# Batch 1's query scaling on VectorE alone, masked-score products in two passes around the fence, and a first matmul pair ahead of block 0's second-half outputs

## The chip, the cores and the metric

The kernel runs on one core of one Trainium2 chip. That core has five engines with a queue of their own each: TensorE (PE, whose weight loads are listed as PEld), VectorE (DVE), ScalarE (ACT), GpSimd (POOL) and SyncE (SP, which here issues nearly all DMAs). An engine works through its instructions in program order and waits for the others by semaphores. The metric is the device time of one execution in microseconds (us), lower is better; the kernel before takes 295.61 us (median of three runs).

## The reference, cut to what matters

A retention layer without a softmax (8 batches, 8 heads, 576 positions, head size 64), whose output is fed to a two-layer network with the activation h * sigmoid(beta * h):

```
gamma = 1 - 2 ** (-5 - arange(H))
Dmat  = where(i >= j, gamma[h] ** (i - j), 0)          # i, j: positions
attn  = ((q @ k.T) / sqrt(64) * Dmat) @ v              # per batch and head
x     = attn, rows (batch, position), columns (head, 64)   # 4608 x 512
h     = x @ w_in                                       # 512 -> 2048
out   = (h / (1 + exp(-beta * h))) @ w_out             # 2048 -> 512
```

## The kernel before, in words

The decay gamma ** (i - j) is split into a factor on the query row (`gq`), a factor on the value row (`gv`, `gvh`) and a 0/1 mask. Queries multiplied by `gq` are called `qs`, values multiplied by their factor `vn`, keys cast to bf16 `kn`. The sequence of a batch is cut into chunks of 64 positions. Inside a chunk the kernel forms masked scores `R` (TensorE product in PSUM, then a VectorE multiplication by the mask, line 493) and multiplies them with `vn`. Everything before the chunk comes in through a running state of 64 x 64 per head: products of `kn` and `vn` (line 504), summed chunk by chunk on VectorE (line 512), cast to bf16 (`sbd`, `sbq`, `end`) and multiplied with the transposed queries `qT`. Both contributions are accumulated in the same PSUM banks `O`, which are then copied to `xT`, the transposed input of the network.

The work stands in nine blocks of 512 rows: one for the first 512 positions of each batch u = 0 to 7, and one (u = 8 in the attention code) for the last 64 positions of all eight batches. A block's network part is 64 `up` matmuls (lines 719 and 734, into `ph`, each group ending in an activation on ScalarE into `gT`) and 64 `down` matmuls (line 754, into `po`), all 128 x 128 by 512 columns. The attention part of a later block is threaded between the network matmuls of an earlier one.

The order is written out by hand. `merged` takes a list `fill` of steps, mostly groups of network matmuls, and streams of pairs (place in the list, step); before step n of `fill` it issues all stream steps whose place is at most n. The order of issue is the program order of every engine; nothing reorders it later. Three places matter here.

**Block 0's second half.** Block 0's own attention runs first, from line 790 on. Its output has two halves, pairs of heads 0 and 1 and pairs 2 and 3. `s_cross(c, a)` (line 418) adds the state's part of half a with two 128 x 128 by 128 matmuls, and `s_x` (line 425) copies one bank of the half to `xT`, one on ScalarE and one on VectorE. The function `rest` (line 846) issues `s_cross` for chunks 1 to 3 of half 1 (six matmuls), both copies, two casts of `w_in` and a reciprocal. It stands at place 1, after the first step of `fill`. That step, `ups(0, (0, 1), 0, ...)`, has four network matmuls which read half 0 of `xT`; the next step has four more on half 0, and the third, `ups(0, (0, 1), 1, ...)`, is the first that reads half 1.

**Batch 1's queries.** `pre_q(b, n)` (line 279) makes a quarter of `qs`. Calls n = 0 and 1 take heads 0 to 3 and n = 2 and 3 heads 4 to 7, each for two of the four position groups. For batch 1 the calls 2 and 3 consist of two instructions each, for even and odd heads, because the heads are exchanged in pairs (`turned`, line 274). All are on VectorE but the second one of n = 3, which is on GpSimd. Then `t_q(1, 0)` and `t_q(1, 1)` (line 343) transpose `qs` on TensorE, eight transposes each, and a copy (line 348) gives `qT`. GpSimd's next instructions are the casts of batch 1's first keys (`o_pre`, line 574).

**The outputs of blocks 2 to 8.** `d_out(u)` (line 519) issues 64 matmuls of 64 x 64 by 64 with `R` and `vn` (line 533), called the own products here, and then the state's part in two halves, `cross(0)` and `cross(1)` (line 546), 28 matmuls each (32 in u = 8). The four 64 x 64 tiles of TensorE work side by side. The own products and `cross(0)` write any given region of `O` from one and the same half of the array's rows, `cross(1)` from the other half. So `cross(1)` must not run into own products that are still on their way into the same region. A fence does that: a one-column VectorE memset (line 537) waits for the last own product, and the first two matmuls of `cross(1)` wait for the memset:

```
        fence = nc.vector.memset(fenced[:], 0.0)
        after(fence, last)
```

For u = 2 to 6, `outputs` (line 955) puts the 32 state matmuls of the next block (`d_st`) between `cross(0)` and `cross(1)`; it does so while the block is built, by running `d_out`, then `chain = d_st(u + 1, 0)`, and then `cross(1)`. For u = 7 and u = 8 nothing stands between them. Block 1's second half has an output function of its own, `half_out` (line 676), in which the own products already stand in two passes of 16 with the fence behind the first pass.

Of the kernel before, what the change touches and what calls it, by code (L numbers as in the profile page):

```python
# [19 lines left out]
def kernel(  # L20
# [10 lines left out]
    nc = tc.nc  # L31
# [5 lines left out]
    HP = H // 2  # L37
# [3 lines left out]
    CB = MB // P  # L41
# [28 lines left out]
    QB = 1  # L70
    HT = MB // 2
    VB = 4
    q_tiles, kv_tiles = {}, {}
# [92 lines left out]
    for x in range(2):  # L166
        t = causal_span[x * D:(x + 1) * D]
        nc.gpsimd.affine_select(out=t, in_=t, pattern=[[-1, 2], [1, CB], [CB, PC]], compare_op=ALU.is_ge,
                                fill=0.0, base=0, channel_multiplier=-2)
# [8 lines left out]
    fenced = consts.tile([P, 1], F32, name="fenced")  # L178
# [28 lines left out]
    def cast_w_in(g, kos=None, pool=()):  # L207
        t = wts[g]
        f0, fn, rows = pieces[g]
        for ko in kos or range(rows[0].start, rows[-1].stop):  # L210
            if ko % 2 == 0 or ko in pool:
                nc.gpsimd.tensor_copy(w_in_sb[:, ko, f0:f0 + fn], t[:, ko])  # L212
                continue
            nc.vector.tensor_copy(w_in_sb[:, ko, f0:f0 + fn], t[:, ko])
# [48 lines left out]
    def xt(m):  # L263
        if m not in xts:
            xts[m] = xpool.tile([P, HP, CB, P], BF16, name="xT", tag="xT" if m < B else "xTt", bufs=2 if m < B else 1)
        return xts[m]

    state_ps = {}
    batch, pair, live, vns = {}, {}, {}, {}
# [4 lines left out]
    turned = [(slice(0, HP), slice(0, HP)), (slice(HP, H, 2), slice(HP + 1, H, 2)), (slice(HP + 1, H, 2), slice(HP, H, 2))]  # L274

    def head_of(b, p, j):
        return 2 * p + (j if b is not None and b < QB or p < 2 else 1 - j)

    def pre_q(b, n):

        if n == 0:
            batch[b] = dict(qs=sb.tile([P, CB, H, D], BF16, name="qs", tag="qs", bufs=2),
                            qT=sb.tile([P, CB, HP, P], BF16, name="qT", tag="qT", bufs=2))
        if b < 2:
            hs, cs = slice(n // 2 * HP, (n // 2 + 1) * HP), slice(n % 2 * 2, n % 2 * 2 + 2)
            for e, (to, hs) in zip((nc.vector, nc.gpsimd if n == 3 else nc.vector), [(hs, hs)] if n < 2 or b < QB else turned[1:]):
                e.tensor_tensor(batch[b]["qs"][:, cs, to], q_tiles[b][:, hs, cs].rearrange("p h i d -> p i h d"),  # L287
                                        gq[:, cs, hs].unsqueeze(3).to_broadcast([P, 2, len(range(H)[hs]), D]), ALU.mult)
        else:
            if n % 2:  # L290
                return
            cs = slice(n, n + 2)
            for to, hs in turned:
                nc.gpsimd.tensor_tensor(batch[b]["qs"][:, cs, to], q_tiles[b][:, hs, cs].rearrange("p h i d -> p i h d"),  # L294
                                        gq[:, cs, hs].unsqueeze(3).to_broadcast([P, 2, len(range(H)[hs]), D]), ALU.mult)
# [54 lines left out]
    spread = [(0, 0), (1, 1), (0, 1), (1, 0)]  # L350

    def half(x):
        return slice(x * D, (x + 1) * D)
# [64 lines left out]
    def s_cross(c, a):  # L418

        for pl in range(2):  # L420
            p = 2 * a + pl
            nc.tensor.matmul(s_view(s_Os[a][c % 2][:, c // 2, pl, :]), sbds[c - 1][:, p, :], s_q(c, slice(0, P), p),
                             start=False, stop=True, skip_group_check=True)

    def s_x(a, hh, e):
        e(xt(0)[:, 2 * a:2 * a + 2].rearrange("k p i (s h w) -> k (p i) s h w", s=2, h=2)[:, :, :, hh, :],
          s_Os[a][hh].rearrange("k s p (i w) -> k (p i) s w", i=CB))
# [30 lines left out]
    def piece(u, c):  # L458

        return live[u * CB + c // 2]  # L460

    def q_of(u, c, j, p):

        if u == B:
            return piece(u, c)["qkT"][half(j), 0, p, half(c % 2)]
        w = TL // CB
        return batch[u]["qT"][half(j), :, p, c * w:(c + 1) * w]

    def columns(u, o):
        return o if u == B else o.rearrange("k (i s) -> k i s", i=CB)  # L470

    def after(later, earlier):
        tc.add_manual_dep(later.ins, earlier.ins.name, mybir.DependencyInfo(mybir.DependencyClass.Sync, mybir.DependencyReason.DATA))
# [45 lines left out]
    def d_out(u):  # L519

        shape = [P, 2, CB, TL] if u == B else [P, 2, CB, CB, TL // CB]
        O = {(hh, y): psum.tile(shape, F32, name="O", tag="sc" if y else "O", bufs=2) for y in range(2) for hh in range(2)}

        def to(c, p, x):
            o = O[c % 2, p // 2][half(x), p % 2]
            return o[:, c // 2] if u == B else o[:, :, c // 2]

        R = batch[u]["R"]
        for cc in range(CB):
            for p in range(HP):  # L530
                for hh, j in spread:
                    h = head_of(u, p, j)
                    last = nc.tensor.matmul(to(2 * cc + hh, p, h % 2), piece(u, 2 * cc)["vn"][half(hh), h, :],  # L533
                                            columns(u, R[cc // 2][half(hh), j, cc % 2, p, :]),
                                            start=cc == 0 and p % 2 == 0, stop=False, skip_group_check=True)

        fence = nc.vector.memset(fenced[:], 0.0)
        after(fence, last)

        def cross(flip):  # L540
            for n, (cc, pp, y, j) in enumerate((cc, pp, y, j) for cc in range(CB) for pp in range(2) for y in range(2) for j in range(2)):
                c, p = 2 * cc + (j ^ flip), pp + 2 * y
                if u < B and c == 0:
                    continue
                s = ends[c] if u == B else sbq[c - 1]
                m = nc.tensor.matmul(to(c, p, j ^ y), s[half(j), p, :], q_of(u, c, j, p),  # L546
                                     start=False, stop=True, skip_group_check=True)
                if flip and n < 2:
                    after(m, fence)

        cross(0)

        def evict():
            for n, ((hh, y), o) in enumerate(O.items()):
                x = xt(u)[:, 2 * y:2 * y + 2]
                if u == B:
                    x, o = x[:, :, :, half(hh)].rearrange("k p c q -> k (p c) q"), o.rearrange("k p c q -> k (p c) q")
                else:
                    x = x.rearrange("k p i (c h s) -> k (p i) c h s", c=CB, h=2)[:, :, :, hh, :]
                    o = o.rearrange("k p i c s -> k (p i) c s")  # L560
                (nc.scalar.copy if n % 2 else nc.vector.tensor_copy)(x, o)  # L561
        return lambda: cross(1), evict
# [159 lines left out]

    phs = {}

    def ups(m, fs, u, banks):

        if m not in gts:
            gts[m] = sb.tile([P, FO, CB, P], BF16, name="gT", tag="gT", bufs=2)
        if u == 0:
            for f, tag in zip(fs, banks):  # L730
                phs[f] = psum.tile([P, MB], F32, name="ph", tag=tag, bufs=dict(mm=3, O=2, sc=2, st=1)[tag])
        kos = (2 * u, 2 * u + 1)
        for ko, f in [(ko, f) for ko in kos for f in fs] if u == 0 or len(fs) == 2 else [(ko, f) for f in fs for ko in kos]:
            nc.tensor.matmul(phs[f][:], w_in_sb[:, ko, f * P:(f + 1) * P], xts[m][:, ko],  # L734
                             start=(ko == 0), stop=(ko == KO - 1))
            if ko == KO - 1:
                nc.scalar.activation(gts[m][:, f], phs[f][:], ACT.Silu, scale=beta_sb[:, f:f + 1])  # L737
# [46 lines left out]
    def F(f, *a):  # L784
        return lambda: f(*a)
# [60 lines left out]
    def rest():  # L846
        for c in range(1, CB):
            s_cross(c, 1)
        s_x(1, 0, act)
        s_x(1, 1, dve)  # L850
        cast_w_in(1, (2, 3))
        nc.vector.reciprocal(rbeta_sb[:], beta_sb[:])
# [5 lines left out]
    def last_state():  # L858
        for a in range(2):
            s_keep(a, 3, (dve, dve), 1 - a)  # L860

    fill = [F(ups, 0, (fo, fo + 1), u, tags) for u in range(2) for fo, tags in ((0, ("mm", "mm")), (2, ("O", "O")))]
    fill += [F(ups, 0, (4, 5), u, ("sc", "sc")) for u in range(2)]
    fill += [F(up, 0, fo) for fo in (6, 7)]
    for fo, tags in ((8, ("O", "O", "sc", "sc")), (12, ("mm", "mm", "mm", "st"))):
        for u in range(2):
            fill += [F(ups, 0, range(fo, fo + 4), u, tags), lambda: None]
    d0 = len(fill)
# [50 lines left out]
    def triangles():  # L919
        for t, pattern in zip(tri, ([[1, CB], [CB, TL // CB]], [[1, TL]])):  # L920
            nc.gpsimd.memset(t[:], 1.0)
            for x in range(2):
# [1 line left out]
                nc.gpsimd.affine_select(out=t[w], in_=t[w], pattern=pattern, compare_op=ALU.is_ge,  # L924
                                        fill=0.0, base=0, channel_multiplier=-1)

    streams = [[(d0 + 2, F(triangles)), (1, rest), (2.5, F(last_products)), (3.6, F(last_state))], [(0, F(load_w_out, 0)), (1.6, F(cast_w_in, 2)), (2.1, F(cast_w_in, 3)), (2.2, F(load_w_out, 1)),
                (4.1, F(cast_w_in, 4)), (6.1, F(cast_w_in, 5)), (6.2, F(load_w_out, 2)), (8.1, F(cast_w_in, 6)),
                (10.1, F(cast_w_in, 7)), (10.2, F(load_w_out, 3))],
               [(d0 - 4 + 3.3 * g, F(cast_w_out, g)) for g in range(WG)],  # L930
# [100 lines left out]
```

## Time and profile before

| | us |
|---|---|
| median of three runs | 295.61 (295.37 to 295.71) |
| the profiled execution, own time | 295.49 |
| its span on the core | 293.8 |
| TensorE matmuls busy | 284.9 (97%) |
| VectorE busy | 104.9 (36%) |
| ScalarE busy | 145.9 (50%) |
| GpSimd busy | 110.5 (38%) |

Times in the trace count from the start of the span. The profiled execution took 295.49 us, 1.7 us more than its span, and 0.12 us less than the median. A line of the timeline gives the start, the time from the first start to the last end, the engine, the source line, the operation, the tiles written and read, the shape and the number of instructions merged into it. Matmuls are pipelined, so that one lasts longer than the distance to the next; distances between starts are what counts on TensorE. The records of some matmuls are missing (55 of the 56 of line 734 are there).

### The profile page before, as it was taken

Reading aid. Unit: us, or ns where it says so; the run is one execution under the profiler, and the core shown is the slowest. Engines: PE = TensorE matmul, PEld = TensorE weight load, DVE = VectorE, ACT = ScalarE, POOL = GpSimd, SP = SyncE. Lnnn points to the kernel's source line nnn. Section 1 sums busy time; section 2 is a strip of 40 time slices with the busy share of each in tenths; the row PEclk is TensorE's granted clock in tenths of the full one; section 3 lists DMA queues with packets and bytes.
Section 4 is the critical chain, followed back from the end, with each engine's and each line's share of the span. In section 5 each row is a group of like instructions: output and inputs, shape, how many; then the busy total and the mean of one; then the engine's idle time right before and its main releaser. Section 6 shows DMA issues by size and latency. Waiting matters only on the chain.

```text
span 293.8 us, 7934 instructions
## 1 busy us (share of the span) xinstructions
PE 284.9 (97%) x3373; PEld 147.1 (50%) x3404; DVE 104.9 (36%) x222; ACT 145.9 (50%) x262; POOL 110.5 (38%) x220
## 2 busy tenths in 40 slices
PE   7899999999999999999999999999999999999995
PEld 2554456885544554455445544554554544444443
DVE  5864566606620650065104520453053500110012
ACT  5556537882387335743473348434780168007600
POOL 3956047944730924371329505773313000000000
PEclk9999999999999999999999999999999999999999
DMA  7999999999999999939999949989997110131011
GB/s 226 305 367 386 377 271 268 209 154 241 231 150 253 271 203 242 243 63 167 229 238 211 185 123 249 193 177 208 208 164 138 74 38 0 36 71 38 0 71 71
DMA packets 121986, 53.99 MB, mean 184 GB/s; under 512 B 97744, under 2 KB 114400, under 8 KB 121952
## 3 DMA queue, kind: packets, MB, share of 16 engines
q1 hardware_dynamic: 121920, 53.49, 82.6%
q8 instruction: 26, 0.43, 0.6%
q14 instruction: 8, 0.07, 0.1%
q10 hardware_dynamic: 32, 0.01, 0.0%
HBM read 36.71 MB, written 9.44 MB: 157 GB/s over the span
## 4 chain that ended last, share of the span: by engine, by line
PE 84%; DMA 10%; SPq 3%; issue 1%; DVE 1%; POOL 0%
PE po L754 39%; PE ph L719 37%; DMA qn<-in_q_dram 4%; DMA wt<-in_moe_w_out_dram 3%; DMA wt<-in_moe_w_in_dram 2%; SPq L104 2%; PE sc L486 2%; PE O L533 2%; PE st L504 1%; PE O L546 1%; DVE qs L287 1%; SPq L204 1%; PE ph L886 0%; SPq L84 0%; PE sc L609 0%
## 5 line engine op out<-in xcount | busy, mean ns | idle before, releaser
L754 PE MATMUL po<-w_out_sb,gT 128*128 128x512 bf16 (+2 forms) x573 | 125.1, 373 | 2.4 <-issue 2.1
L721 ACT ACTIVATE gT<-ph,beta_sb 128x512 bf16<-128x512 f32 (+1 forms) x144 | 91.4, 643 | 48.3 <-PE ph L719 47.9
L719 PE MATMUL ph<-xT,w_in_sb 128*128 128x512 bf16 (+1 forms) x566 | 113.1, 356 | 0.5
L754 PEld LDWEIGHTS <-gT 128*128 128x128 bf16 x593 | 56.1, 98 | 63.9
L719 PEld LDWEIGHTS <-w_in_sb 128*128 128x128 bf16 x576 | 56.0, 98 | 55.1 <-DVE first L512 0.3
L761 DVE COPY ot<-po 128x512 f32<-128x512 f32 (+2 forms) x33 | 22.2, 672 | 72.8 <-PE po L754 70.0
L493 DVE TENSOR_TENSOR R<-sc,tri 128x512 bf16<-128x512 f32 x30 | 18.7, 683 | 61.5 <-PE sc L486 61.5
L294 POOL TENSOR_TENSOR qs<-qn,gq 128x256 bf16<-128x256 f32 (+1 forms) x36 | 26.4, 763 | 36.9 <-DMA qn<-in_q_dram 36.9
L323 POOL CAST kn<-kvn 128x128 bf16<-128x128 f32 (+1 forms) x78 | 22.8, 331 | 31.4 <-DMA kvn<-in_k_dram 31.3
L301 POOL TENSOR_TENSOR vn<-kvn,gv 128x512 bf16<-128x512 f32 x26 | 27.0, 1044 | 6.3 <-DMA kvn<-in_v_dram 6.0
L561 ACT CAST xT<-O 128x512 bf16<-128x512 f32 x14 | 7.5, 589 | 31.9 <-PE O L546 31.9
L516 ACT CAST sbd<-warm 128x256 bf16<-128x256 f32 x18 | 7.3, 405 | 25.7 <-DVE warm L512 20.7
L734 PE MATMUL ph<-xT,w_in_sb 128*128 128x512 bf16 x55 | 12.9, 379 | 0.1
L512 DVE TENSOR_TENSOR warm<-st,first 128x256 f32<-128x256 f32 x20 | 8.4, 422 | 9.6 <-PE st L504 8.4
L512 DVE TENSOR_TENSOR first<-st,warm 128x256 f32<-128x256 f32 x25 | 10.6, 425 | 2.5
L561 DVE CAST xT<-O 128x512 bf16<-128x512 f32 x14 | 9.0, 686 | 4.9 <-PE O L546 4.9
L737 ACT ACTIVATE gT<-ph,beta_sb 128x512 bf16<-128x512 f32 x14 | 8.7, 687 | 4.2 <-PE ph L734 4.2
L311 POOL TENSOR_TENSOR kn<-tln,gq 128x128 bf16<-128x128 f32 (+1 forms) x12 | 5.7, 471 | 11.8 <-DMA tln<-in_q_dram 6.5
L212 POOL CAST w_in_sb<-wt 128x256 bf16<-128x256 f32 (+1 forms) x15 | 8.0, 546 | 4.9 <-DMA wt<-in_moe_w_in_dram 4.9
L516 ACT CAST sbd<-first 128x256 bf16<-128x256 f32 x18 | 7.3, 405 | 2.3 <-DVE first L512 0.3
L734 PEld LDWEIGHTS <-w_in_sb 128*128 128x128 bf16 x56 | 5.2, 98 | 6.3 <-issue 0.5
L229 DVE TENSOR_SCALAR w_out_sb<-wt,rbeta_sb 128x512 bf16<-128x512 f32 x13 | 5.9, 484 | 5.0 <-DMA wt<-in_moe_w_out_dram 5.0
(132 smaller groups left out, 166.4 us busy)
## 6 DMA issues: line engine op xcount, KB each, us to landing
qn<-in_q_dram SPq DMA_DIRECT2D x16, 512.0 KB, 6.2
kvn<-in_k_dram SPq DMA_DIRECT2D x32, 256.0 KB, 5.8
kvn<-in_v_dram SPq DMA_DIRECT2D x32, 256.0 KB, 5.3
out_dram<-ot SPq DMA_DIRECT2D x31, 256.0 KB, 3.6
wt<-in_moe_w_out_dram SPq DMA_DIRECT2D x8, 512.0 KB, 9.2
wt<-in_moe_w_in_dram SPq DMA_DIRECT2D x5, 512.0 KB, 10.2
wt<-in_moe_w_in_dram SPq DMA_DIRECT2D x6, 256.0 KB, 6.9
tln<-in_q_dram SPq DMA_DIRECT2D x8, 128.0 KB, 4.6
```

Source lines behind the costliest of these rows:

```text
L294: nc.gpsimd.tensor_tensor(batch[b]["qs"][:, cs, to], q_tiles[b][:, hs, cs].rearrange("p h i d -> p i h d"), gq[:, cs, hs].unsqueeze(3).to_ ...
L301: nc.gpsimd.tensor_tensor(live[i]["vn"], kv_tiles.pop(i)[:, 1], gains(gv, c), ALU.mult)
L323: nc.gpsimd.tensor_copy(kn[:, c % 2, to], t[:, 0, hs])
L493: nc.vector.tensor_tensor(R[x][:, j].rearrange("k c p q -> k (c p) q"), sc[x, j].rearrange("k c p q -> k (c p) q"), mask, ALU.mult)
L512: nc.vector.tensor_tensor(new[:], add, sums[(c - 1) % 2][:], ALU.add)
L516: e((sbq[c] if c < NC - 1 else ends[u])[:], new[:])
L561: (nc.scalar.copy if n % 2 else nc.vector.tensor_copy)(x, o)
L719: nc.tensor.matmul(ph, w_in_sb[:, ko, fo * P:(fo + 1) * P], xts[m][:, ko, :, w], start=(ko == 0), stop=(ko == KO - 1))
L721: nc.scalar.activation(gts[m][:, fo, :, w], ph, ACT.Silu, scale=beta_sb[:, fo:fo + 1])
L734: nc.tensor.matmul(phs[f][:], w_in_sb[:, ko, f * P:(f + 1) * P], xts[m][:, ko], start=(ko == 0), stop=(ko == KO - 1))
L754: nc.tensor.matmul(po[:, x:y], gT[:, fo, ms, :], w_out_sb[:, fo, n0 + x:n0 + y], start=(fo == 0), stop=(fo == FO - 1), skip_group_check=m < 2)
L761: (nc.scalar.copy if m == 0 else nc.vector.tensor_copy)(ot, po[:, :nn])
```

## The change

It has three parts.

1. In `pre_q`, all scaling instructions of batches 0 and 1 go to VectorE. One instruction moves: the last of batch 1, 128 x 256 elements, from GpSimd to VectorE.
2. In `d_out`, the 64 own products are issued in two passes of 32. The first pass has the products whose regions `cross(1)` will write, the second those that `cross(0)` will write. The fence stands between the passes. `cross` is unchanged.
3. The first step of `fill` is split: two of its four matmuls, then `rest`, then the other two. `ups` gets an argument `one` for that. The rest of the order stays.

```
@@ pre_q
-            for e, (to, hs) in zip((nc.vector, nc.gpsimd if n == 3 else nc.vector), [(hs, hs)] if n < 2 or b < QB else turned[1:]):
-                e.tensor_tensor(batch[b]["qs"][:, cs, to], q_tiles[b][:, hs, cs].rearrange("p h i d -> p i h d"),
+            for to, hs in ([(hs, hs)] if n < 2 or b < QB else turned[1:]):
+                nc.vector.tensor_tensor(batch[b]["qs"][:, cs, to], q_tiles[b][:, hs, cs].rearrange("p h i d -> p i h d"),
@@ d_out
-        for cc in range(CB):
-            for p in range(HP):
-                for hh, j in spread:
-                    h = head_of(u, p, j)
-                    last = nc.tensor.matmul(to(2 * cc + hh, p, h % 2), piece(u, 2 * cc)["vn"][half(hh), h, :],
-                                            columns(u, R[cc // 2][half(hh), j, cc % 2, p, :]),
-                                            start=cc == 0 and p % 2 == 0, stop=False, skip_group_check=True)
-
-        fence = nc.vector.memset(fenced[:], 0.0)
-        after(fence, last)
+        for other in range(2):
+            for n in range(32):
+                cc, pp, y, hh = n // 8, n // 4 % 2, n // 2 % 2, n % 2
+                p, j = pp + 2 * y, hh if other else 1 - hh
+                h = head_of(u, p, j)
+                last = nc.tensor.matmul(to(2 * cc + hh, p, h % 2), piece(u, 2 * cc)["vn"][half(hh), h, :],
+                                        columns(u, R[cc // 2][half(hh), j, cc % 2, p, :]),
+                                        start=cc == pp == 0, stop=False, skip_group_check=True)
+            if not other:
+                fence = nc.vector.memset(fenced[:], 0.0)
+                after(fence, last)
@@ ups
-    def ups(m, fs, u, banks):
+    def ups(m, fs, u, banks, one=None):
-        if u == 0:
+        if u == 0 and not one:
-        kos = (2 * u, 2 * u + 1)
+        kos = (2 * u, 2 * u + 1) if one is None else (2 * u + one,)
@@ fill and streams
-    fill = [F(ups, 0, (fo, fo + 1), u, tags) for u in range(2) for fo, tags in ((0, ("mm", "mm")), (2, ("O", "O")))]
+    fill = [lambda: (ups(0, (0, 1), 0, ("mm", "mm"), 0), rest(), ups(0, (0, 1), 0, None, 1))]
+    fill += [F(ups, 0, (fo, fo + 1), u, tags) for u, fo, tags in ((0, 2, ("O", "O")), (1, 0, None), (1, 2, None))]
-    streams = [[(d0 + 2, F(triangles)), (1, rest), (2.5, F(last_products)), (3.6, F(last_state))], ...
+    streams = [[(d0 + 2, F(triangles)), (2.5, F(last_products)), (3.6, F(last_state))], ...
```

More of the change, by code (lines that the diff above doesn't have):

```diff
@@ L925, in triangles @@
                                         fill=0.0, base=0, channel_multiplier=-1)
-    streams = [[(d0 + 2, F(triangles)), (1, rest), (2.5, F(last_products)), (3.6, F(last_state))], [(0, F(load_w_out, 0)), (1.6, F(cast_w_in, 2)), (2.1, F(cast_w_in, 3)), (2.2, F(load_w_out, 1)),
+    streams = [[(d0 + 2, F(triangles)), (2.5, F(last_products)), (3.6, F(last_state))], [(0, F(load_w_out, 0)), (1.6, F(cast_w_in, 2)), (2.1, F(cast_w_in, 3)), (2.2, F(load_w_out, 1)),
                 (4.1, F(cast_w_in, 4)), (6.1, F(cast_w_in, 5)), (6.2, F(load_w_out, 2)), (8.1, F(cast_w_in, 6)),
```

## The prediction, made before the changed kernel had run

> **What bounds the kernel.** I read the page's busy shares first, then the list of waits, then the timeline at the three places that the change touches.
>
> ```profile
> PE 284.9 (97%) x3373; PEld 147.1 (50%) x3404; DVE 104.9 (36%) x222; ACT 145.9 (50%) x262; POOL 110.5 (38%) x220
> ...
> PE T L347 <- DVE qs L287: 1.2, 4, 0.4
> ```
>
> TensorE is busy for 97% of the span, and its longest listed wait for another engine after the start is the 0.4 us for `qs` at the transposes of line 347. So a saving counts only where TensorE itself stops, and such stops are short. They have to be read from distances between starts, because the modelled ends hide them.
>
> Place one, block 0's second half, on TensorE:
>
> ```profile
> 15.76 1.04 PE L734 MATMUL ph<-xT,w_in_sb 128*128 128x512 bf16 x3
> 16.63 0.50 PE L422 MATMUL O<-qT,sbd 128*128 128x128 bf16 x6
> 16.97 2.06 PE L734 MATMUL ph<-xT,w_in_sb 128*128 128x512 bf16 x8
> 18.96 0.44 PE L439 MATMUL st<-vn,kn 64*64 64x64 bf16 x16
> 19.33 2.76 PE L734 MATMUL ph<-xT,w_in_sb 128*128 128x512 bf16 x12
> 21.93 0.38 PE L719 MATMUL ph<-xT,w_in_sb 128*128 128x512 bf16 x1
> ```
>
> From 19.33 to 21.93 twelve matmuls take 2.60 us, 0.217 each. From 16.97 to 18.96 eight take 1.99, where 8 x 0.217 = 1.73, plus some 0.10 for the turn to small matmuls (77.14 to 77.44 is 0.30 for one matmul and such a turn), gives 1.83: a stop of about 0.16. It lies before the third step, which needs half 1 of `xT`; VectorE's copy of that half runs from 17.17 to 17.86, when the eight are half done.
>
> Place two, batch 1's queries:
>
> ```profile
> 40.09 0.43 DVE L287 TENSOR_TENSOR qs<-qn,gq 128x256 bf16<-128x256 f32 x1 [0.25 <-DMA qn<-in_q_dram]
> 40.20 0.79 POOL L287 TENSOR_TENSOR qs<-qn,gq 128x256 bf16<-128x256 f32 x1 [11.28 <-DMA qn<-in_q_dram]
> 40.43 0.84 DVE L287 TENSOR_TENSOR qs<-qn,gq 128x256 bf16<-128x256 f32 x1
> 41.00 0.73 POOL L574 CAST kn<-kvn 128x512 bf16<-128x512 f32 x1
> 41.19 0.82 DVE L287 TENSOR_TENSOR qs<-qn,gq 128x256 bf16<-128x256 f32 x1
> ...
> 40.93 0.83 PE L347 MATMUL T<-ident,qs 128*128 128x128 bf16 x12
> 42.16 0.38 PE L347 MATMUL T<-ident,qs 128*128 128x128 bf16 x4 [0.40 <-DVE qs L287]
> ```
>
> TensorE issues twelve transposes and stops for the last four until VectorE's third instruction ends at 42.01; they begin 0.15 later, at 42.16. Four transposes take 0.22 (42.16 to 42.38), twelve 0.65, so TensorE could have gone on at about 41.59: the stop is 0.57. VectorE's start is set by the queries' landing, which also ended GpSimd's wait of 11.28.
>
> Place three, the fence, in u = 7 and u = 8:
>
> ```profile
> 218.00 0.71 PE L533 MATMUL O<-R,vn 64*64 64x64 bf16 x64
> 218.54 0.38 PE L546 MATMUL O<-qT,sbd 64*64 64x64 bf16 x23
> 218.81 0.06 DVE L537 MEMSET fenced<- 128x1 f32 x1 [2.20 <-PE O L533]
> 218.92 0.40 PE L546 MATMUL O<-qT,sbd 64*64 64x64 bf16 x24
> ...
> 231.93 0.83 PE L546 MATMUL O<-kT,end 64*64 64x64 bf16 x64
> 232.21 0.06 DVE L537 MEMSET fenced<- 128x1 f32 x1 [0.88 <-PE O L533]
> 232.92 0.59 PE L754 MATMUL po<-w_out_sb,gT 128*128 128x512 bf16 x2 [0.16 <-issue]
> ```
>
> In u = 7 the memset ends at 218.87, 0.33 after the last own product was issued, and TensorE goes on at 218.92. `cross(0)` has 28 matmuls from 218.54. In u = 2 the same 28 take 0.24 (77.99 to 78.23), so TensorE was done at 218.78 and stopped for 0.14. In u = 8 the 64 cross matmuls reach to the next network matmul at 232.92; taking off the missing record (0.22) and the turn back (0.12) leaves 0.65, and 64 at 0.24/28 are 0.55: a stop of 0.10. In u = 2 to 5 the 32 state matmuls between take another 0.29, and no stop is to be seen.
>
> **The change part by part.** The sums are against the profiled execution's 295.49 us, which is 0.12 below the median of the runs; I carry the difference over to the median at the end.
>
> *Block 0's second half.* Nothing is added. Two of the first four matmuls change places with six `s_cross` matmuls, which start 0.43 earlier, at about 16.20. They need `sbd`, whose last two casts end at 15.84 and 15.89; even with 0.15 for the signal that is 16.04. VectorE's copy then starts at about 16.75, just as the small `beta` instructions ahead of it end (16.57 + 0.17), ScalarE's at 16.63, and the half is there at 17.45 + 0.15 = 17.60. TensorE asks for it after two steps, at 17.83. So the stop of 0.16 goes and nothing takes its place; the bounds are 0 and 0.16, and even a late `sbd` would only give some of it back. `rest` also holds two casts of `w_in` and a reciprocal, whose order on VectorE and GpSimd stays; the casts at 17.81 and 17.84 follow a load (GpSimd idled 1.34 for it), so they do not move, and neither does SyncE's next issue, at 18.39 on the casts' end. No DMA is moved. But the gain ends at 41.6: TensorE arrives at the last four transposes 0.16 earlier and stops 0.16 longer, because VectorE's start hangs on a load. Its worth at the end is **0**. If that load came 0.57 earlier, it would be worth its 0.16.
>
> *Batch 1's queries.* VectorE gets four instructions in place of three. The first took 0.43, its follower started 0.34 after it. Numbers two and three took 0.84 and 0.82, and each ended 0.28 after a GpSimd instruction did (40.99 to 41.27, 41.73 to 42.01). So an instruction beside GpSimd seems to wait for GpSimd's to end. Without the moved one, GpSimd idles until its cast of `kn`; that stood right behind, so its load landed by 41.0, but not much earlier: half of q, 512 KB, lands some 1.5 after the other half (38.55 to 40.09 by VectorE's starts), so 256 KB of keys take 0.75, to about 40.85. VectorE's first two then end at 40.86, the third starts at 40.77 and is ahead of the cast, the cast runs to about 41.65 (40.85 or 41.0 plus 0.61 to 0.73), and the fourth ends 0.28 later. I take **41.95, a gain of 0.06**. Bounds: four undisturbed ones end at 40.09 + 3 x 0.34 + 0.43 = 41.54, a gain of 0.47. Three slowed ones, 0.76 apart as the second and third were, end at 42.77, a loss of 0.76. The trace stands nearest to the middle, because GpSimd has work from 41.0 on and none before. The following casts of keys do not come sooner: they idled 0.17 for their load until 41.91. If TensorE gained the whole 0.47, those casts (to 42.66) would be its next wait, at 42.79, and would just not hold it.
>
> [...]
>
> *The own products.* The count stays 64 per block. The new order is that of `half_out`, whose 32 take 0.28 (55.50 to 55.78), 8.7 ns each; the old order takes 0.55 for 64 (77.44 to 77.99), 8.6 ns. I take 0; over seven blocks, 0.01 per pass of 32 either way gives ±0.1. The memset now waits for the 32nd product, so it ends 0.33 after that one, while 32 products and 28 or 32 cross matmuls (0.27 + 0.24 = 0.51) go on. The stops of 0.14 and 0.10 go: **0.24**. Less than 0 would need the fence on VectorE to be late: it idled 2.20 and 0.88 ahead of the two fences, and what stands behind on its queue is the copy of the same `O`, which waits for `cross(1)` anyway. The upper end is 0.24, the stops themselves; the lower 0, if the stops are not the fence's. What the first pass reads of `R` and `vn` it reads up to 0.14 sooner. `R` was made before VectorE's preceding copy of `ot`, at 230.64 in u = 8, and GpSimd, which makes `vn`, is idle from the 30th slice of the page on.
>
> *Sum:* 0 + 0.06 + 0.24 = 0.30 off 295.49, that is 295.19; on the scale of the median, 295.61 - 0.30 = **295.3 us**.
>
> **The rivals.**
>
> *The fourth instruction costs nothing, 294.9.* If VectorE runs unhindered because the keys land late, or because the slowness had another cause, the queries gain 0.47: 295.61 - 0.47 - 0.24 = 294.90. For it: the first instruction took 0.43 though GpSimd's began during it. Against: both slow ones end by GpSimd's clock, and the cast still stands in their time. Chance 0.12.
>
> *The fourth is one more slow one, 296.1.* GpSimd's casts then lie beside three of four: 0.76 later at the transposes, 0.24 back at the fences, 295.61 + 0.52 = 296.13. It decides from a loss of 0.24 on. For it: VectorE's single instruction of line 570 also took 0.73 beside GpSimd. Against: GpSimd has nothing to do before the keys land. Chance 0.10.
>
> *The new order of the own products runs slower: slower than before.* Place: the 7 x 64 products of line 533. If the array's halves followed each other less well, at the 13 ns per matmul of u = 7's cross stretch (0.75 for 56), 64 would cost 0.28 more and seven blocks 2.0: 297.3. From 0.04 a block on it eats up the rest, and from 0.13 a block on it shows as slower. For it: consecutive products now go to four banks in place of two. Against: `half_out` does the same at 8.7 ns. Chance 0.08.
>
> *The stops are not the fence's, 295.5.* Breaks like them could come from the array or its instruction supply. For it: the chain of waits has 0.39 and 0.45 for u = 6's cross halves where u = 2 to 4 have 0.25 or so, and the fence there was in time. Against: in u = 7 and 8 the break comes within 0.06 of the memset's end, or is of that size. Then only 0.06 is left: 295.55. Chance 0.13.
>
> **How the numbers follow.** My forecast has 0.50, its own range 295.0 to 295.6 by the ±0.1 of the products, the breaks of u = 6 (0.14 + 0.20, which may come and go) and the runs' own spread. The rivals have 0.12, 0.10, 0.08 and 0.13; 0.07 is left for what I don't see. From 294.8 to 296.2 all but the third rival and the unseen are held, about 0.85. About 0.2%, 0.6 us, is what a measurement of this kernel can tell from no change: faster is below 295.02, slower above 296.20. Faster: the first rival and 0.08 of the forecast, if u = 6's breaks go too, 0.20. Slower: the third rival, 0.03 of the second and 0.04 unseen, 0.15. Within: 0.65.
>
> **What would show it.** In the changed kernel's timeline: eight matmuls of line 735 in a row at 0.217 (stop gone), and the transposes' stop longer than 0.57; four VectorE instructions of `qs`, the last ending near 41.95, and the cast of `kn` starting near 41.0; `cross(1)` in u = 7 and 8 following `cross(0)` without a break, with the memset over before. Wrong would make me: transposes restarting later than 42.4 or earlier than 41.8, own products of more than 0.57 for 64, or a break left at `cross(1)`.

## The result, and the profile after

The changed kernel takes 295.21 us (median of 22 runs), the kernel before 295.83 beside it on the same chip: a ratio of 0.9983, interval 0.9975 to 0.9992. One of the 22 runs took 1042.89 us; it is in the median (295.19 without it) and not in the ratio. The ratio on record is not the quotient of the two medians, which would be 0.9979. So the changed kernel is 0.17% faster here, which is less than the 0.3% by which one and the same kernel differed between two sessions further down. The profiled execution took 295.01 us with a span of 293.3, against 295.49 and 293.8.

The busy shares of the changed kernel, then what TensorE waited for (us in total, times, longest; all lines of the list):

```profile
PE 288.1 (98%) x3404; PEld 147.4 (50%) x3404; DVE 104.5 (36%) x223; ACT 145.9 (50%) x262; POOL 109.8 (37%) x219
```

```profile
PE ph L240 <- DVE warm L134: 1.1, 1, 1.1
PE T L380 <- POOL kn L373: 0.5, 2, 0.3
PE st L445 <- POOL vn L373: 0.3, 1, 0.3
PE T L380 <- POOL kn L371: 0.2, 1, 0.2
```

No matmul record is missing here (3404 of 3404), so the higher busy time of PE says nothing by itself. The wait of the transposes (line 347) for VectorE's `qs` has left the list. The three places, in the changed kernel's timeline (start, length to the last end, engine, line, operation, tiles, count):

```profile
16.16 0.60 PE L735 MATMUL ph<-xT,w_in_sb 128*128 128x512 bf16 x2
16.60 0.50 PE L422 MATMUL O<-qT,sbd 128*128 128x128 bf16 x6
16.93 2.32 PE L735 MATMUL ph<-xT,w_in_sb 128*128 128x512 bf16 x10
19.19 0.44 PE L439 MATMUL st<-vn,kn 64*64 64x64 bf16 x16
...
40.10 0.42 DVE L287 TENSOR_TENSOR qs<-qn,gq 128x256 bf16<-128x256 f32 x1 [0.23 <-DMA qn<-in_q_dram]
40.44 0.42 DVE L287 TENSOR_TENSOR qs<-qn,gq 128x256 bf16<-128x256 f32 x1
40.78 0.42 DVE L287 TENSOR_TENSOR qs<-qn,gq 128x256 bf16<-128x256 f32 x1
41.10 0.90 POOL L575 CAST kn<-kvn 128x512 bf16<-128x512 f32 x1 [12.20 <-DMA kvn<-in_k_dram]
41.11 0.42 DVE L287 TENSOR_TENSOR qs<-qn,gq 128x256 bf16<-128x256 f32 x1
41.16 1.06 PE L347 MATMUL T<-ident,qs 128*128 128x128 bf16 x16
...
217.61 0.71 PE L534 MATMUL O<-R,vn 64*64 64x64 bf16 x64
218.15 0.39 PE L547 MATMUL O<-qT,sbd 64*64 64x64 bf16 x22
218.15 0.06 DVE L538 MEMSET fenced<- 128x1 f32 x1 [1.91 <-PE O L534]
218.39 0.49 PE L547 MATMUL O<-qT,sbd 64*64 64x64 bf16 x20
...
230.98 0.71 PE L534 MATMUL O<-R,vn 64*64 64x64 bf16 x64
231.51 0.73 PE L547 MATMUL O<-kT,end 64*64 64x64 bf16 x64
231.52 0.06 DVE L538 MEMSET fenced<- 128x1 f32 x1 [0.60 <-PE O L534]
232.18 1.04 PE L755 MATMUL po<-w_out_sb,gT 128*128 128x512 bf16 x4
```

*Place one.* From 16.93 to 19.19 ten network matmuls take 2.26, which is 10 x 0.216 and the turn of 0.10: the stop of 0.16 is gone. This run's first network matmul started 0.40 later than in the profile before (16.16 against 15.76), and the matmuls of line 439 only 0.23 later.

*Place two.* All four VectorE instructions took 0.42, the last ended at 41.53, and sixteen transposes stand in a row without a stop. GpSimd's cast began 0.01 before the fourth, while VectorE's third still ran (40.78 to 41.20), and took 0.90 in place of the 0.61 that casts of this size take elsewhere in this trace (line 371). Here the slowed one is GpSimd. The keys' load landed at 40.98, 0.90 after that of the queries (40.08), and GpSimd began 0.12 after it.

*Place three.* In u = 8 the 64 cross matmuls take 0.67 less the turn back of 0.12, so 0.55: the stop of 0.10 is gone, and the memset was over at 231.58, 0.07 after the first of them. In u = 7 the memset ended at 218.21; a break of 0.10 that remains in `cross(1)`, at 218.53, comes 0.32 later and is not the fence's. Whether `cross(1)` has to wait for the own products at all is not shown: every kernel here has that wait.

*What is new.* Block 1's second half, whose code was not touched. Its 32 own products after, in the timeline:

```profile
54.94 0.42 DVE L512 TENSOR_TENSOR end<-st,warm 128x256 bf16<-128x256 f32 x1
55.16 0.69 PE L691 MATMUL O<-R,vn 64*64 64x64 bf16 x32
```

The same two rows in the kernel before:

```profile
54.93 0.42 DVE L512 TENSOR_TENSOR end<-st,warm 128x256 bf16<-128x256 f32 x1
55.50 0.45 PE L690 MATMUL O<-R,vn 64*64 64x64 bf16 x32
```

Before, the products started at 55.50 and took 0.45. Now the first one is issued at 55.16 and the second only at 55.41. The bank that the products write is held by the state sums of that block (line 499 takes it under the same tag, `O`), and a chain on VectorE has to read them first. The chain's last instruction is the line 512 shown: it ends at 55.36, 0.05 before TensorE goes on, and the semaphore that the second product waits for rises with it, at 55.37.

Where the time went in this pair of profiles, by start times on TensorE, after less before:

| point on TensorE | before | after | difference so far |
|---|---|---|---|
| first network matmul of line 734 / 735 | 15.76 | 16.16 | +0.40 |
| line 439, block 0 | 18.96 | 19.19 | +0.23 |
| last four transposes of batch 1's `qs` | 42.16 | 41.83 | -0.34 |
| network matmul after block 1's second half | 56.27 | 56.18 | -0.10 |
| own products of u = 5 | 164.82 | 164.67 | -0.15 |
| own products of u = 7 | 218.00 | 217.61 | -0.39 |
| span | 293.8 | 293.3 | -0.5 |

Of 0.34 gained at the transposes 0.24 was given back at block 1's second half. From there to u = 7 another 0.29 appears where no part of the change promised anything: the profile before has breaks of 0.12 in the state products and scores ahead of u = 5's outputs and of 0.09 and 0.16 in u = 6's outputs, of which only 0.07 is there after. u = 7 and u = 8 give the remaining 0.13. So in these two profiles the largest single item is none of the change's.

### The profile page after: what moved, and what is told of

It is laid out like the page before. It is cut to its first block, busy times and chain, and to the rows that moved or that the text cites. A ratio compares the mean times of both kernels' runs of the same rounds, so it can differ in the third digit from the quotient of the medians.

```text
span 293.3 us, 7964 instructions
## 1 busy us (share of the span) xinstructions
PE 288.1 (98%) x3404; PEld 147.4 (50%) x3404; DVE 104.5 (36%) x223; ACT 145.9 (50%) x262; POOL 109.8 (37%) x219
## 4 chain that ended last, share of the span: by engine, by line
PE 95%; DMA 2%; POOL 1%; SPq 1%; issue 0%; DVE 0%; POOLq 0%
PE po L755 43%; PE ph L720 38%; PE ph L735 4%; DMA kvn<-in_k_dram 2%; PE sc L486 2%; PE O L534 2%; PE st L504 1%; PE O L547 1%; POOL kn L373 1%; PE st L445 1%; PE O L414 0%; SPq L104 0%; POOL vn L373 0%; PE ph L888 0%; SPq L84 0%; PE T L347 0%
## 5 line engine op out<-in xcount | busy, mean ns | idle before, releaser
L755 PE MATMUL po<-w_out_sb,gT 128*128 128x512 bf16 (+2 forms) x593 | 128.6, 373 | 0.0
```

What stands on the lines that cost most here:

```text
L755: nc.tensor.matmul(po[:, x:y], gT[:, fo, ms, :], w_out_sb[:, fo, n0 + x:n0 + y], start=(fo == 0), stop=(fo == FO - 1), skip_group_check=m < 2)
```

## The experiments

They ran in three sessions of four kernels, each session on another chip, and each kernel beside the kernel before, whose median there was 295.7 to 295.8. Ratios below are to the kernel before in the same session, with the 95% interval. As in the result, they are not the quotients of the medians.

### Each part alone, and all again

Part 1 alone (the hunk of `pre_q` on the kernel before):

```
-            for e, (to, hs) in zip((nc.vector, nc.gpsimd if n == 3 else nc.vector), ...):
-                e.tensor_tensor(batch[b]["qs"][:, cs, to], ...
+            for to, hs in ([(hs, hs)] if n < 2 or b < QB else turned[1:]):
+                nc.vector.tensor_tensor(batch[b]["qs"][:, cs, to], ...
```

> Part 1 alone: batch 1's query scaling all on VectorE, everything else as before. Theory N (next wait): the stop of 0.57 at the last four transposes nearly goes, because VectorE's four instructions run undisturbed and end at about 41.55, and TensorE leaves the transposes some 0.45 earlier; but block 1's second-half outputs cannot begin before about 55.40, when VectorE's chain of states gives its PSUM bank back, where the kernel before arrives at 55.50. So a break of about 0.35 stands behind the first product there, and only 0.10 is left: about 0.1 us faster, ratio 0.9997. Theory G (the gain goes through): no such break, 0.45 us faster, ratio 0.9985. Theory P (my prediction's sum): 0.06 us, and a fourth instruction that ends near 41.95.

Measured: 295.11 us, 0.9967 (0.9954 to 0.9979, five runs; against the session's median of 295.80 it would be 0.9977). The first row below is the state's cast beside GpSimd, which took 0.29 where the changed kernel has 1.02, the last the 32 products of block 1's second half, without a break:

```profile
52.64 0.29 DVE L516 CAST sbd<-warm 128x256 bf16<-128x256 f32 x1
52.65 1.18 POOL L294 TENSOR_TENSOR qs<-qn,gq 128x512 bf16<-128x512 f32 x1
53.30 0.68 DVE L516 CAST sbd<-first 128x256 bf16<-128x256 f32 x1
55.12 0.45 PE L690 MATMUL O<-R,vn 64*64 64x64 bf16 x32
```

The same rows of the changed kernel:

```profile
52.52 1.04 POOL L294 TENSOR_TENSOR qs<-qn,gq 128x512 bf16<-128x512 f32 x1
52.69 1.02 DVE L516 CAST sbd<-warm 128x256 bf16<-128x256 f32 x1
54.08 0.29 DVE L516 CAST sbd<-first 128x256 bf16<-128x256 f32 x1
```

In the changed kernel GpSimd started 0.17 ahead of the cast, and the cast ended 0.15 after GpSimd did. With part 1 alone the cast came 0.01 first and lost nothing. The chain then ended at 54.98 in place of 55.36, and TensorE's whole advance passed.

Part 2 alone (the hunk of `d_out`: two passes, fence between them):

```
-        for cc in range(CB):
-            for p in range(HP):
-                for hh, j in spread:
+        for other in range(2):
+            for n in range(32):
...
+            if not other:
+                fence = nc.vector.memset(fenced[:], 0.0)
```

> Part 2 alone: the own products in two passes with the fence between, everything else as before. Theory P (my sum): the stops of 0.14 in u = 7 and 0.10 in u = 8 go, nothing else moves, 0.24 us faster, ratio 0.9992. Theory C (the new order has a price): the break of u = 8 goes (0.10), and in u = 2 to 6 each block loses about 0.02, because cross(0) takes 0.27 in place of 0.24 behind the second pass while the own products take 0.01 less; together about 0.1 us faster, ratio 0.9996. If breaks in the 64 x 64 stretches of u = 5 to 7 come and go by themselves, some of them (0.07 to 0.16 each) will lie elsewhere than in the kernel before.

Measured: 295.83 us, 0.9994 (0.9984 to 1.0005). Part 2 shows no gain that can be told from none, though the stops at the fences went. A break of 0.26 at block 1's second half is here too, without part 1.

Part 3 alone (the first step of `fill` split around `rest`):

```
+    fill = [lambda: (ups(0, (0, 1), 0, ("mm", "mm"), 0), rest(), ups(0, (0, 1), 0, None, 1))]
-    streams = [[(d0 + 2, F(triangles)), (1, rest), (2.5, F(last_products)), ...
+    streams = [[(d0 + 2, F(triangles)), (2.5, F(last_products)), ...
```

> Part 3 alone: two of the first four matmuls ahead of block 0's second-half outputs, the other two behind, everything else as before. Theory P (my sum): the stop of 0.16 before the third step goes, TensorE comes to the transposes 0.16 earlier and stops there 0.16 longer, 0.73 in place of 0.57; time the same, ratio 1.0000. Rival (the saving lasts): TensorE leaves the transposes earlier by 0.16 too, ratio 0.9995.

Measured: 295.77 us, 0.9992 (0.9983 to 1.0002).

```profile
40.83 0.85 PE L347 MATMUL T<-ident,qs 128*128 128x128 bf16 x12
42.12 0.38 PE L347 MATMUL T<-ident,qs 128*128 128x128 bf16 x4 [0.44 <-DVE qs L287]
```

TensorE arrives at the transposes at 40.83, 0.10 earlier than before, and the last four come 2.08 after VectorE's first instruction on that half of q, which is the figure of the kernel before to the last digit. Block 0 started 0.08 later in this profile, which took half of the 0.16. The distance from the twelfth to the thirteenth transpose grew from 0.62 to 0.66: the stop has only moved.

The changed kernel again, in the same session:

> The changed kernel itself, to be compared with its parts on the same chip. If the parts add up, its gain is the sum of the three runs beside it: by theory N and C about 0.2 us (ratio 0.9993), by theory G and P about 0.7 us (0.9976). The runs already made gave 0.5 us (0.9983, 0.9975 to 0.9992).

Measured: 295.40 us, 0.9981 (0.9973 to 0.9990). The three parts alone add up to a gain of 0.0047 there and the whole has 0.0019, so they don't add. With the 0.9997 that part 1 alone gave in the next session they would add up to 0.0017.

### The parts in pairs, the queries again, and the order without the early fence

Parts 1 and 2, without the split of `fill`:

> Parts 1 and 2, without the early matmul pair. If part 2 is worth what it takes away less what it adds (stops of 0.10 and 0.14 at the fences gone, five blocks 0.02 longer each): 0.14 us faster than part 1 alone, 0.0005 in the ratio. If the own products' order costs more than the fence gives, it is slower than part 1 alone, as the changed kernel was beside it (295.40 against 295.11).

Measured: 295.25 us, 0.9980 (0.9970 to 0.9989). That is 0.0017 below part 1 alone in the same session (0.9997, below), where 0.0005 was expected; the two intervals overlap.

Parts 1 and 3, without the passes:

> Parts 1 and 3, without the two passes. With part 1 TensorE no longer stops long at the transposes, so the 0.16 saved before them can now last as far as VectorE's end at 41.5 lets it: theory L (lasts): 0.1 us faster than part 1 alone. Theory M (my prediction, for the kernel before): the load of the queries sets the transposes in any case, the same as part 1 alone.

Measured: 295.58 us, 0.9994 (0.9983 to 1.0005).

```profile
40.85 1.24 PE L347 MATMUL T<-ident,qs 128*128 128x128 bf16 x16
```

These sixteen transposes do contain a stop, of 0.17: TensorE was early, and the last four came 1.49 after VectorE's start on that half. So 1.49 is VectorE's limit with part 1, against 2.08 without it. The ratio is too near to part 1 alone in the same session (0.9997) to decide between the two theories.

Part 1 alone once more:

> Part 1 alone once more, beside the pairs with part 2 and part 3. Theory Q (part 1 carries the change): 0.4 us of stop less at the transposes (four undisturbed instructions end at 41.5 instead of 42.0), ratio 0.9965 to 0.9985, as the first time (0.9967). Rival (the first time was a lucky draw of its breaks): ratio 0.9990 or more.

Measured: 295.83 us, 0.9997 (0.9983 to 1.0012, twelve runs). The same program gave 0.9967 in the session before, on another chip, and the two intervals don't overlap. What an interval covers is the scatter within a session; whether the chip or the session made the difference is not shown. The profiled execution took 296.57 and shows one place where 1.3 us went, in the own products of u = 2, which part 1 doesn't touch:

```profile
77.15 0.70 PE L533 MATMUL O<-R,vn 64*64 64x64 bf16 x61
79.11 0.22 PE L533 MATMUL O<-R,vn 64*64 64x64 bf16 x3 [1.26 <-issue]
```

The 61st to 64th product, a break of 1.45, "issue": no engine, no DMA and no semaphore that the profile shows. The same break, 0.65 long, is in the profiled execution of part 3 alone:

```profile
77.40 0.70 PE L533 MATMUL O<-R,vn 64*64 64x64 bf16 x61
78.57 0.22 PE L533 MATMUL O<-R,vn 64*64 64x64 bf16 x3 [0.47 <-issue]
```

The new order with the fence behind the second pass, on the kernel before:

```
+        for other in range(2):
+            for n in range(32):
...
+            if other:
+                fence = nc.vector.memset(fenced[:], 0.0)
+                after(fence, last)
```

> The kernel before with the own products in the new order of two passes, and the fence left behind the last of them. It has the price of the order without the gain of the fence. Theory C: blocks 2 to 5 take 1.465 in place of 1.442 from the first own product to the next network matmul, so the order alone costs about 0.1 us over five blocks, and u = 7 and 8 keep their stops of 0.14 and 0.10 behind cross(0); ratio 1.0004. If the longer blocks come from the fence's new place instead, blocks 2 to 5 take 1.442 here and the ratio is 1.0000.

Measured: 295.79 us, 0.9997 (0.9988 to 1.0005). The stops at `cross(1)` of u = 7 and 8 stay, 0.14 and 0.12. Here is u = 3 in this kernel, with `cross(0)` at 105.48 and the state matmuls of the next block behind it:

```profile
104.94 0.71 PE L534 MATMUL O<-R,vn 64*64 64x64 bf16 x64
105.48 0.37 PE L547 MATMUL O<-qT,sbd 64*64 64x64 bf16 x21
105.73 0.48 PE L504 MATMUL st<-vn,kn 64*64 64x64 bf16 x32
105.78 0.06 DVE L538 MEMSET fenced<- 128x1 f32 x1 [0.90 <-PE O L534]
```

and in the changed kernel:

```profile
104.15 0.71 PE L534 MATMUL O<-R,vn 64*64 64x64 bf16 x64
104.69 0.40 PE L547 MATMUL O<-qT,sbd 64*64 64x64 bf16 x21
104.96 0.48 PE L504 MATMUL st<-vn,kn 64*64 64x64 bf16 x32
104.70 0.06 DVE L538 MEMSET fenced<- 128x1 f32 x1 [0.60 <-PE O L534]
```

The own products take 0.54 in both, and `cross(0)` 0.25 with the late fence and 0.27 with the early one, whose memset runs just as `cross(0)` begins. From the first own product to the last small matmul of u = 3 to 5 it is 1.316 in the kernel before, 1.314 in the new order with the late fence, and 1.340 in the changed kernel. The new order costs nothing; the early fence costs 0.024 in a block that had no stop to lose. How a fence does that is not shown.

### A busy GpSimd beside the four, and the chain behind the break

Part 1, and an extra GpSimd product where its own had stood:

```
+            if b == 1 and n == 3:
+                nc.gpsimd.tensor_tensor(span_of(1, 0)["vn"][:, :, :2], q_tiles[b][:, hs, cs]..., gq..., ALU.mult)
```

> Part 1 alone, but GpSimd still makes the same product of 128 x 256 in the same place, as extra work whose result nobody uses (it goes into a tile that GpSimd fills later). VectorE has four instructions as in part 1 alone, GpSimd is as busy as before. Theory X (VectorE waits out whatever GpSimd runs): the second and third of VectorE's four take about 0.8 again, and the last transposes begin some 2.4 to 2.9 after VectorE's first instruction, where part 1 alone had 1.5 and the kernel before 2.08. Rival (the exchange of even and odd heads made these two instructions slow, or the loads): four times 0.42, transposes at 1.5.

Measured: 296.06 us, 1.0003 (0.9989 to 1.0018).

```profile
40.19 0.43 DVE L287 TENSOR_TENSOR qs<-qn,gq 128x256 bf16<-128x256 f32 x1 [0.24 <-DMA qn<-in_q_dram]
40.31 0.79 POOL L290 TENSOR_TENSOR vn<-qn,gq 128x256 bf16<-128x256 f32 x1 [11.30 <-DMA qn<-in_q_dram]
40.53 0.84 DVE L287 TENSOR_TENSOR qs<-qn,gq 128x256 bf16<-128x256 f32 x1
41.12 0.72 POOL L577 CAST kn<-kvn 128x512 bf16<-128x512 f32 x1
41.30 0.83 DVE L287 TENSOR_TENSOR qs<-qn,gq 128x256 bf16<-128x256 f32 x1
42.05 0.63 DVE L287 TENSOR_TENSOR qs<-qn,gq 128x256 bf16<-128x256 f32 x1
42.73 0.40 PE L350 MATMUL T<-ident,qs 128*128 128x128 bf16 x4 [0.91 <-DVE qs L287]
```

With GpSimd busy VectorE's second to fourth take 0.84, 0.83 and 0.63 in place of 0.42, and the transposes come 2.54 after VectorE's start in place of 1.49. So it was GpSimd's work beside them, and nothing in VectorE's own instructions, that made two of three slow before; and part 1 gains by emptying GpSimd's queue, not by the engine that does the work.

The changed kernel with one state cast of block 1's second half on ScalarE, to shorten the chain that holds the bank:

```
-        chain((4, 5, 6, 7), dve)
+        chain((4,), act)
+        chain((5, 6, 7), dve)
```

> The changed kernel with the first bf16 cast of batch 1's second state chain on ScalarE instead of VectorE (line 516 for chunk 4, called from late_scores). That cast took 0.29 on VectorE where GpSimd was idle and 0.67 to 1.02 where GpSimd multiplied the next queries. Theory N (the chain holds the PSUM bank that block 1's second-half outputs wait for): the chain ends at 55.1 or earlier in every run, and the break of 0.22 to 0.29 behind the first product, which three of six kernels with part 1 had, is gone; on average 0.1 us faster than the changed kernel. Rival: the break stays, because something else is waited for.

Measured: 296.27 us, 1.0018 (1.0006 to 1.0029), slower than the kernel before beside it.

```profile
52.70 0.41 ACT L516 CAST sbd<-warm 128x256 bf16<-128x256 f32 x1 [1.70 <-DVE warm L512]
53.53 2.78 PE L720 MATMUL ph<-xT,w_in_sb 128*128 128x256 bf16 x24 [0.96 <-ACT gT L722]
56.24 0.44 PE L691 MATMUL O<-R,vn 64*64 64x64 bf16 x32
```

The break at the 32 products is gone, but TensorE comes 1.08 later than in the changed kernel: ScalarE now waits 1.70 for VectorE's sum with its activations queued behind, and TensorE waits 0.96 for a bank that an activation has to free. Nor did the chain get shorter: it ended at 55.32 (55.36 in the changed kernel, 55.1 expected), because two of the casts left on VectorE took 0.76 and 0.68 beside GpSimd. The experiment doesn't tell whether a shorter chain alone would give the 0.25 back.

That kernel with the early fence for u = 7 and 8 only:

```
-            if not other:
+            if other == (u < B - 1):
```

> As the kernel with the state cast on ScalarE, and the fence stands between the passes only in u = 7 and 8, where no state matmuls follow cross(0); in u = 2 to 6 it stands behind the second pass. Theory C: blocks 2 to 5 take 1.440 in place of 1.465, u = 8 keeps its 1.20; 0.12 us faster than the kernel beside it, the best of all by the trace. Rival: the early fence was not what made these blocks longer, and they stay at 1.465.

Measured: 296.44 us, 1.0019 (1.0006 to 1.0031). By the same distances u = 3 to 5 take 1.313 against 1.339 in the kernel without this edit, and u = 8 keeps its short form (1.074, where the late fence has 1.175). So the price is the early fence's, seen twice. What it comes to over u = 2 to 6, five times 0.024 or 0.12, is below what the total can tell: the kernel is not faster than the one beside it (296.27).

The changed kernel a third time:

> The changed kernel once more, for the comparison with the two variants beside it: ratio 0.9975 to 0.9990, as in the two times before (0.9983 and 0.9981). It has the early fence (blocks 2 to 5 at 1.465) and may or may not have the break behind block 1's first second-half product.

Measured: 295.57 us, 0.9997 (0.9987 to 1.0008), outside the range expected. Over its three sessions the changed kernel stands at 0.9983, 0.9981 and 0.9997, 0.9987 on average. No kernel here beats it and the kernel before beyond the scatter between sessions.

## Why the prediction was right, and where its terms were not

The forecast of 295.3 us and a gain of 0.30 holds for the total: the three ratios average to a gain of 0.38 (0.0013 x 295.8), with 0.1 and 0.6 as the single sessions' ends. That it came so near is in good part luck. The 295.21 was measured beside 295.83 for the kernel before, where the forecast started from 295.61. And of the three terms only the first stands as it was worked out: the second was too low by 0.42 at VectorE, the third too high by about 0.14, and 0.24 was lost in the profile at a place that the sum doesn't have.

*Block 0's second half, 0: right for the kernel before.* The stop is absent in all seven profiles with the split and stands at 0.16 in all seven without it. In part 3 alone the transposes' stop grew by 0.04 and the total didn't move beyond its interval (0.9983 to 1.0002). With part 1 beside it the cover thins. In five profiles with part 1, the changed kernel's three among them, TensorE arrives too late at the transposes to be stopped there (the last four come 1.68 to 2.33 after VectorE's start on that half); in four they come at 1.48 to 1.50, in three of these behind a stop of 0.14 to 0.21. Whether the 0.16 counts in the changed kernel thus depends on how late block 0 starts, which differs by up to 0.9 between profiles (first network matmul at 15.76 to 16.62, once at 17.13). Before, the long stop took such a late start in. Now it is passed on to the next place.

*Batch 1's queries, 0.06: too low by 0.42 at VectorE.* The third started ahead of the cast as forecast (40.78 for 40.77). The step that failed is "and the fourth ends 0.28 later", behind the cast. The keys' load was put at 40.85; it landed at 40.98, and GpSimd began the cast only at 41.10. By then VectorE's fourth could start too, and it won: it ended at 41.53, within 0.01 of the lower bound of 41.54 that I had kept for "undisturbed". This fits my first rival ("because the keys land late"), to which I gave 0.12. No run moved the load, so whether an earlier landing would have let the cast win stays open. In every profile with part 1 and no extra product the four took 0.42 each and the cast, begun within 0.02 of the fourth's start, took 0.87 to 0.91. By their ends, the slowed one of the two ran as if it waited for the other. The cast ended 0.47 after VectorE's fourth, VectorE's slowed instructions of the kernel before 0.28 after GpSimd's, and the state's cast of 1.02 ended 0.15 after GpSimd's. Each is 0.14 less than the slowed instruction takes undisturbed (0.61, 0.42 and 0.29), so all but 0.14 of it lies behind the other's end. I had counted with that only against VectorE. How the one holds up the other is not shown, nor why VectorE's fourth won even where the cast had started 0.02 earlier.

The rival's time of 294.9 was still not reached. TensorE's gain at the transposes was 0.34: the stop of 0.57 and the 0.16 of place one, less 0.40 by which block 0 started later. Of the 0.34, 0.24 was lost again at block 1's second half. There a second term was missing altogether. In the profile before, the state chain ended at 55.35 and TensorE came at 55.50, 0.15 behind, so any advance of more than about 0.1 met it. In five of fourteen profiles (the changed kernel twice, part 2 alone, both pairs of parts) the first product is followed by a break of 0.08 to 0.29, and in all five the second product comes 0.05 to 0.06 after the chain's last instruction ends. In the other nine TensorE comes at least 0.06 after that end, and there is no break. The prediction looked at GpSimd's key casts as the next wait and didn't look for the next bank.

*The own products and the fence, 0.24: the mechanism right, the sum more than twice too high.* From the first own product to the last small matmul, u = 8 takes 1.074 where it took 1.179 before. For u = 7, whose other breaks come and go, the mean is 1.11 over seven profiles with the early fence and 1.23 over seven without. That is 0.10 and 0.12, so 0.22 in all. The missing term is the early fence's price in u = 2 to 6, where no stop was to be gained: 5 x 0.024 = 0.12 (measured in u = 3 to 5; in u = 6 breaks hide it). The step was "I take 0; over seven blocks, 0.01 per pass of 32 either way gives ±0.1", which priced the order and not the fence's new place. Net about 0.10, which alone can't be told from none (part 2 alone: 0.9994).

*The rivals.* "The new order of the own products runs slower" is false: with the late fence a block takes 1.439 to the next network matmul, 1.442 in the old order. "The stops are not the fence's" is false for u = 8 and for u = 7's break behind the memset, but it named something real: u = 7 keeps a break of 0.10 in `cross(1)` long after its fence. "The fourth is one more slow one" needs a GpSimd that is busy; with the extra product it happened, though smaller than priced (2.54 - 2.08 = 0.46 later; I had 0.76). A reading beside it was off: GpSimd is idle from the 32nd slice of the page on, not the 30th, so it still worked at times beside u = 7. No term hung on that.

*What stays open.* Breaks come and go in the small matmuls, mostly of u = 5 to 7 (distances of 0.06 to 0.19 between two matmuls), and made more than half of the difference between the two profiles shown. Their cause wasn't found. One and the same kernel (part 1 alone) differed by 0.3% between two sessions on two chips, which is 0.9 us and more than the 0.38 itself. So the traces show which stops went and which came, but not how much of the 0.38 is the change's own.

## What to carry to other kernels

A stop in front of a point that hangs on a load, like the 0.57 here, also takes in late starts. Shortening it makes the kernel's time follow them, and the gain can end at the next resource, here a PSUM bank that a VectorE chain frees (0.24 of the 0.34 went there): find the arrival there before counting it. Two engines that slow each other, as VectorE's products (0.84 in place of 0.42) and GpSimd's cast (0.90 in place of 0.61) did here, should be read for both outcomes of an even race, and for what the loser holds up. An early fence was worth its place only where there was a stop to remove (0.10 in u = 8, against a price of 0.024 in each of u = 3 to 5), and a gain of a tenth of a per cent needs several sessions, not a narrow interval from one.

## What the runs showed of the hardware that was not expected

The break among the 64 own products of u = 2 goes with the fetch of instructions. The page of the changed kernel lists two queues of the kind "instruction"; this is the larger:

```profile
q8 instruction: 26, 0.43, 0.6%
```

These are 26 fetches with 0.43 MB in all, 16 KB each. In the fourteen profiles, the last fetch of that kind begins between 0.62 and 4.90 us before u = 2's first own product. Where it begins 0.62, 1.60, 1.68 and 1.94 before, the break is 1.45, 0.66, 0.67 and 0.22; from 2.06 on there is none. All four breaks stand behind the 61st product, in four different programs, and end 2.58 to 2.84 after the fetch began; no semaphore stands on these instructions. No experiment moved the fetch, so this is an observation over fourteen profiles: that the late fetch causes the break is not shown.

A close race between VectorE and GpSimd decided about 0.4 us in two places (41.53 in place of the forecast 41.95 for the queries, 54.98 in place of 55.36 for the state chain). At the queries VectorE's next instruction won against the cast that started within 0.02 of it, in every profile with part 1 and no extra product.
